# GEMM2 in products of 256 columns, with moving operands 192 bytes beyond the loaded ones

## The chip, the cores and the metric

The kernel runs on one core of one Trainium2 chip. The metric is device time in microseconds for one execution; the median of three runs of the kernel before is 678.66 us (678.33 to 679.98).

## What is computed

Sliding-window attention with sink tokens feeds a two-layer network with a leaky activation. All tensors are float32.

```
scores = q @ k.T / sqrt(64)                      # 4 batches, 8 heads, 768 tokens, head_dim 64
keep   = (key < 4) | (0 <= query - key < 128)    # 4 sink tokens, a window of 128
a      = softmax(where(keep, scores, -1e9))
x      = (a @ v), heads side by side             # 3072 tokens x 512
h      = x @ w_in                                # 512 -> 2048      (GEMM1)
g      = max(h, 0) + alpha * min(h, 0)
out    = g @ w_out                               # 2048 -> 512      (GEMM2)
```

## The kernel before, in words

The 3072 tokens are cut into twelve chunks of 256 (`QC`), three to a batch. For each chunk the attention gives x transposed, features on partitions; it is then taken through the network in sixteen blocks of the hidden layer (`f`, 0 to 15, 128 hidden features each). To keep float32 accuracy with matmuls of a rounded float32 type, every operand is split into a high part and a low part, and a product is the sum of three: high by high, high by low, low by high.

GEMM1 of a block (`gemm1`, matmul at L901) works in four steps of 128 input features. Each step has three products: a 128x128 block of the weights is loaded into TensorE, and 256 columns of x (`xh` or `xl`, 256 tokens) stream past it. Twelve products add up to h in one PSUM bank. ScalarE scales it by alpha (L905), VectorE takes the maximum (L906), ScalarE makes the high part `gh` (L907), VectorE the low part `gl` (L908).

GEMM2 (`gemm2`, L913 on) comes two blocks later. For it g is the loaded operand and the weights stream: for each half `j` of the chunk's tokens a 128x128 block of `gh` or `gl` is loaded, and the block's `w_out` (512 columns, its high part L938 and L936, its low part L939) streams past. There are six products of 512 columns to a block: `gh` by high and `gh` by low for both halves, then, when `gl` is ready, `gl` by high for both. The results accumulate in two PSUM banks over the sixteen blocks. The last block of the last chunk has the same six in another order (L923 to L925), half by half, so that the first output can leave early. After the sixteenth block ScalarE copies each bank to SBUF (L944) and a DMA on SP's queue stores it.

Each product has a load of its own, also where two in a row use the same block: the profile has as many loads as products.

The attention of the next chunk is spread over the blocks of the current one: the scores (L604, L605: 260 columns, 132 in a batch's first tiles) of one head and one half of the queries at a time, the softmax on VectorE and ScalarE, the products with v (L793, L882) towards the end. In the last chunk only the network is left.

The order of all instructions is planned beforehand (`Plan.draw`). An operation is declared by `op(engine, cost, run, reads, writes)`; the planner simulates the engines with these costs, picks each engine's order, and `Plan.emit` chains the instructions of an engine in that order. The cost of a matmul is `mm(columns)`, 0.456 ns a column, and GEMM2 is declared as two operations, of four and of two products of 512 columns.

Where tiles lie: `const` and `main` are pools without rotation that lay tiles one after another, in the order in which they are first asked for, rounded up to 32 bytes. So the sizes of tiles set the addresses of those behind. The size of the tile that holds one block's weights is `ROWS` words: first the split w_in (2 x 512 words), then `HALF` words of padding, then the split w_out. The sixteen weight tiles are in `const`; `gh`, `gl`, `vs`, `kq`, the padding tile `half` and then `xh`, `xl` follow in `main`. The tile `size` is the first of all; the weight tile of f = 14 lies right behind it, ahead of a group of small tiles (896 bytes together), the other fifteen behind those. `kq` holds q high, q low, `HALF` words of padding, and k.

With the kernel's first tile at byte 8320, the addresses modulo 512 come to:

| operand | before |
|---|---|
| w_in of f = 0, 3, 7, 11 | 384 |
| w_in of f = 1, 5, 9 | 128 |
| w_in of f = 2, 6, 10, 14, 15 | 256 |
| w_in of f = 4, 8, 12, 13 | 0 |
| w_out | w_in + 64 |
| gh, gl | 128 |
| xh, xl | 448 |
| q high, q low in the two kq | 128, 256 |
| k | q + 64 |

Steps inside an operand (256 or 128 columns, the four feature steps, high and low part) are multiples of 512 bytes.

Of the kernel before, what the change touches and what calls it, by code (L numbers as in the profile page):

```python
# [9 lines left out]
F32 = mybir.dt.float32  # L10
# [9 lines left out]
P = 128  # L20
B, H, S, D = 4, 8, 768, 64
DM, DF = 512, 2048
NS = 4
WIN = 2 * P + NS
QC = 2 * P
KC = 3 * P + 2 * NS
HALF = 16
KQ = 2 * QC + HALF + KC + HALF // 2
ROW = 2 * DM + HALF
ROWS = 2 * ROW  # L30
CPB = S // QC
NCHUNK = B * CPB
NF = DF // P
# [49 lines left out]
class Plan:  # L83
# [20 lines left out]
    def held(self, tile_):  # L104
        v = Value(None)
        v.at = tile_
        return v

    def op(self, engine, cost, run, reads=(), writes=(), tail=0.09, mode=None, nbytes=0, other=None, locks=False):
        o = Op(engine, cost, tail, run, self.rank if engine == "PE" else None)  # L110
        o.ways = {engine: (cost, run)}
        if other:
            o.ways[other[0]] = other[1:]
        o.born = self.rank
        if engine == "PE":
            self.rank += 1
        o.mode, o.nbytes, o.index = mode, nbytes, len(self.ops)
        seen = []
        for group, writing in ((reads, False), (writes, True)):
            for x in group:  # L120
                v, key = x if isinstance(x, tuple) else (x, None)
                if v not in seen:
                    seen.append(v)
                keys = [k for k in set(v.wrote) | set(v.read) if key is None or k is None or k == key]
                for k in keys:
                    o.before.update(v.wrote.get(k, ()))
                    if writing:
                        o.before.update(v.read.get(k, ()))
                if writing:
                    for k in keys:  # L130
                        if key is None or k == key:
                            v.wrote.pop(k, None)
                            v.read.pop(k, None)
                    v.wrote.setdefault(key, []).append(o)
                else:
                    v.read.setdefault(key, []).append(o)
        for v in seen:
            v.left += 1
        o.values = seen
        o.takes = [v for v in seen if v.kind]  # L140
        o.locks = locks
        self.ops.append(o)
        return o
# [148 lines left out]
def cast(n, psum=False):  # L292
    return (0.045 if psum else 0.092) + 0.84e-3 * n
# [18 lines left out]
def mm(n):  # L312
    return 0.456e-3 * n
# [12 lines left out]
def program(ctx, tc, qk, pairs, vp, vq, vs, w, par, out):  # L326
    nc = tc.nc
    const = ctx.enter_context(tc.tile_pool(name="const", bufs=1))
# [10 lines left out]
    def several(name, n, shape, dtype):  # L339
        plan.kind(name, [pool.tile(shape, dtype, name=f"{name}{i}") for i in range(n)])  # L340
# [7 lines left out]
    several("vs", 1, [P, DM], F32R)  # L348
    several("kq", 2, [P, KQ], F32R)
    pool.tile([P, HALF], F32, name="half")  # L350
    several("xh", 2, [P, KT, QC], F32R)
# [13 lines left out]
    several("jk", 3, [P, 2], F32)  # L365
    several("ts", 1, [P, 2, 4, 32], F32R)

    size = const.tile([P, 2 * NF], F32, name="size")[:, :NF]
    sizes = held(size)
    raws, fins = {}, {}  # L370

    def load_weights(f, engine="ACT"):
        raw = raws[f] = held(None)

        def run():
            raw.at = const.tile([P, ROWS], I32, tag=f"w{f}", name="wraw")[:, :2 * ROW].rearrange("p (i x) -> p i x", i=2)[:, :, :2 * DM]
            (nc.sync if engine == "SP" else nc.scalar).dma_start(
                raw.at, w[f].bitcast(I32).rearrange("i p x -> p i x"))
        return op(engine, ISSUE if engine == "SP" else 0.12, run, writes=[raw] + lent.get(f, []), nbytes=8 * P * 2 * DM)

    def convert_weights(f):
# [23 lines left out]
        def high_part(engine):  # L405
            fin.at = const.tile([P, ROWS], F32R, tag=f"w{f}", name=f"w{f}")[:, :2 * ROW].rearrange(
                "p (i x) -> p i x", i=2)[:, :, :2 * DM].rearrange("p i (a x) -> p i a x", a=2)
            (nc.scalar.copy if engine == "ACT" else nc.vector.tensor_copy)(fin.at[:, :, 0], wf())
# [68 lines left out]
    part, alt = param[:, :4], param[:, 4:].bitcast(F32)  # L477
# [81 lines left out]
    def prep_head(c, h):  # L559
# [5 lines left out]
        kq = val("kq")  # L565
        ks, qh, ql = [lambda s=s: kq.at[:, s] for s in (slice(2 * QC + HALF, 2 * QC + HALF + KC), slice(0, QC), slice(QC, 2 * QC))]
        q_raw, k_raw = lambda: st.at[:, :QC], lambda: st.at[:, QC:]
# [345 lines left out]
    def gemm2(c, f, dst):  # L913
        gh, gl = gs.pop((c, f))
        fin = fins[f]
        if f == 0:
            acc[c] = [val("pa"), val("s")] if c == 1 else [val("o"), val("o")]
        o2 = acc[c]
        if c == NCHUNK - 1 and f == NF - 1:
            for j in range(2):  # L920
                def last(j=j):
                    js = slice(j * P, (j + 1) * P)
                    nc.tensor.matmul(o2[j].at, gh.at[:, js], fin.at[:, 1, 0], start=False, stop=False)  # L923
                    nc.tensor.matmul(o2[j].at, gh.at[:, js], fin.at[:, 1, 1], start=False, stop=False)
                    nc.tensor.matmul(o2[j].at, gl.at[:, js], fin.at[:, 1, 0], start=False, stop=True)  # L925
                op("PE", 3 * mm(DM), last, reads=[fin, gh, gl], writes=[o2[j]], tail=R_TAIL)
                ob = val("ob")
                op("ACT", cast(DM, True), lambda ob=ob, j=j: nc.scalar.copy(ob.at, o2[j].at), reads=[o2[j]], writes=[ob])
                op("ACT", 0.1, lambda ob=ob, j=j: nc.scalar.dma_start(dst(j), ob.at), reads=[ob], nbytes=4 * P * DM)
            return  # L930
        for lowpart in range(2):
            def some(lowpart=lowpart):
                for j in range(2):
                    js = slice(j * P, (j + 1) * P)
                    if lowpart:
                        nc.tensor.matmul(o2[j].at, gl.at[:, js], fin.at[:, 1, 0], start=False, stop=(f == NF - 1))  # L936
                    else:
                        nc.tensor.matmul(o2[j].at, gh.at[:, js], fin.at[:, 1, 0], start=(f == 0), stop=False)  # L938
                        nc.tensor.matmul(o2[j].at, gh.at[:, js], fin.at[:, 1, 1], start=False, stop=False)  # L939
            op("PE", (2 if lowpart else 4) * mm(DM), some, reads=[fin, gl if lowpart else gh], writes=o2, tail=R_TAIL)  # L940
        if f == NF - 1:
            for j in range(2):
                ob = val("ob")
                op("ACT", cast(DM, True), lambda ob=ob, j=j: nc.scalar.copy(ob.at, o2[j].at), reads=[o2[j]], writes=[ob])  # L944
                op("SP", ISSUE, lambda ob=ob, j=j: nc.sync.dma_start(dst(j), ob.at), reads=[ob], nbytes=4 * P * DM)
            del acc[c]
# [112 lines left out]
    def dst(c):  # L1059
        return lambda j: out[c * QC + j * P:c * QC + (j + 1) * P]  # L1060
# [11 lines left out]
    for n, (c, f) in enumerate(order):  # L1072
        convert(f + 2)
        if (c, f) == (NCHUNK - 1, NF // 2):
            judge()
        gemm1(c, f)
        pend.append((c, f))
        todo = work[n]
        cut = round(len(todo) / 2)
        for st in todo[:cut]:  # L1080
            st()
        if len(pend) > LAG:
            gemm2(*pend[0], dst(pend.pop(0)[0]))
        for st in todo[cut:]:
            st()
    for a in pend:
        gemm2(*a, dst(a[0]))
# [197 lines left out]
```

## Time and profile before

| | |
|---|---|
| median of three runs | 678.66 us |
| profiled execution | 678.67 us, its span 676.7 us |
| TensorE products | 664.0 us busy (98%), 4534 |
| TensorE loads | 580.2 us busy (86%), 4534 |
| VectorE | 525.9 us busy (78%) |
| ScalarE | 397.5 us busy (59%) |
| GEMM1 products (L901), 256 columns | 2304 |
| GEMM2 products (L936, L938, L939, L923 to L925), 512 columns | 1152 |

A row of the timeline gives the start in microseconds from the span's start, the length, the engine and line, what is written and read, the shape, and how many instructions in a row were merged. PE is TensorE's products and PEld its loads. Products overlap, so the length of a row is not what a product costs; the difference of the starts of two products in a row is. A row of the windows gives, for each engine, the busy time and the number of instructions in that stretch, then the granted clock and what the DMAs did.

### The profile page before, as it was taken

The page shows a single profiled execution, that of the slowest core. Times are in us where ns is not written, and L with a number is a line of the kernel's source. Part 1 is how long each engine was busy: PE and PEld are TensorE (multiplying, and loading weights), DVE is VectorE, ACT ScalarE, POOL GpSimd, SP SyncE. Part 2 cuts the span into 40 slices and gives each one's busy share as a digit, 9 for nine tenths or more (in the row PEclk, how much of TensorE's full clock was granted, in tenths as well). Part 3 has the DMA queues.
Part 4 walks back from the last instruction along what each step waited for, and adds up shares of the span by engine and source line. Part 5 has one row for each costly group of instructions (what it writes and reads, how often), then busy time and mean ns, then how long its engine had stood idle before and what let it go on. Part 6 is the DMA issues. An engine that isn't in the chain of part 4 may idle for free.

```text
span 676.7 us, 13245 instructions
## 1 busy us (share of the span) xinstructions
PE 664.0 (98%) x4534; PEld 580.2 (86%) x4534; DVE 525.9 (78%) x1750; ACT 397.5 (59%) x1066; POOL 34.6 (5%) x115
## 2 busy tenths in 40 slices
PE   9989999999999999999999999999999999999996
PEld 4568898888989989989988988988998988998995
DVE  6999999968967977986986985995895994994331
ACT  6989888827537627736636735744744753853332
POOL 2110000001000000010000000010000000000000
PEclk9989999999999999999999999999999999999999
DMA  8674641325343453442434433542542543420001
GB/s 313 238 278 163 244 162 44 122 75 155 118 125 107 127 144 105 139 133 88 141 118 118 142 112 92 157 139 61 173 127 77 161 127 89 141 93 18 32 2 35
DMA packets 58683, 85.19 MB, mean 126 GB/s; under 512 B 9072, under 2 KB 35056, under 8 KB 58608
## 3 DMA queue, kind: packets, MB, share of 16 engines
q1 hardware_dynamic: 55056, 71.17, 34.5%
q10 hardware_dynamic: 3552, 13.11, 5.3%
q8 instruction: 37, 0.61, 0.4%
q14 instruction: 38, 0.31, 0.2%
HBM read 67.22 MB, written 17.04 MB: 125 GB/s over the span
## 4 chain that ended last, share of the span: by engine, by line
PE 83%; DVE 9%; ACT 5%; issue 2%; POOL 0%; DMA 0%; ACTq 0%; SPq 0%; POOLq 0%
PE bank L901 35%; PE bank L938 12%; PE bank L936 11%; PE bank L939 11%; PE bank L793 3%; PE bank L605 3%; PE bank L604 3%; PE bank L882 2%; DVE wa L402 2%; ACT pt L621 1%; ACT wa L388 1%; DVE wa L400 1%; DVE w L411 1%; DVE g L906 1%; DVE gl L908 1%
## 5 line engine op out<-in xcount | busy, mean ns | idle before, releaser
L901 PE MATMUL bank<-xh,w 128*128 128x256 f32 x1536 | 307.8, 282 | 0.4 <-DVE g L906 0.2
L901 PEld LDWEIGHTS bank<-xh,w 128*128 128x128 f32 x1536 | 250.2, 189 | 9.5 <-DVE g L906 3.2
L901 PE MATMUL bank<-xl,w 128*128 128x256 f32 x768 | 215.1, 280 | 0.1
L905 ACT ACTIVATE g<-bank,param 128x256 f32<-128x256 f32 x192 | 90.4, 471 | 117.6 <-PE bank L901 112.2
L938 PE MATMUL bank<-w,gh 128*128 128x512 f32 x382 | 151.5, 397 | 0.2 <-ACT gh L907 0.2
L939 PE MATMUL bank<-w,gh 128*128 128x512 f32 x382 | 150.4, 394 | 0.0
L901 PEld LDWEIGHTS bank<-xl,w 128*128 128x128 f32 x768 | 145.1, 189 | 4.4 <-DVE xl L815 0.3
L621 ACT ACTIVATE pt<-pt,nm 128x260 f32<-128x260 f32 (+1 forms) x192 | 94.5, 493 | 53.4 <-DVE nm L617 52.9
L936 PE MATMUL bank<-w,gl 128*128 128x512 f32 x382 | 120.2, 396 | 0.0
L906 DVE TENSOR_TENSOR g<-bank,g 128x256 f32<-128x256 f32 x192 | 79.7, 419 | 51.1 <-ACT g L905 50.3
L907 ACT CAST gh<-g 128x256 fp32r<-128x256 f32 x192 | 77.0, 404 | 60.8 <-DVE g L906 60.6
L908 DVE TENSOR_TENSOR gl<-g,gh 128x256 fp32r<-128x256 f32 x192 | 80.4, 423 | 26.5 <-ACT gh L907 23.0
L617 DVE CUSTOM_DVE_ANT_0 pt<-bank,masks 128x260 f32<-128x260 f32 (+1 forms) x192 | 74.9, 401 | 19.7 <-PE bank L605 16.2
L936 PEld LDWEIGHTS bank<-w,gl 128*128 128x128 f32 x382 | 70.8, 188 | 16.3 <-issue 0.7
L938 PEld LDWEIGHTS bank<-w,gh 128*128 128x128 f32 x382 | 72.0, 188 | 9.5 <-ACT gh L907 0.6
L939 PEld LDWEIGHTS bank<-w,gh 128*128 128x128 f32 x382 | 71.9, 188 | 8.2
L570 DVE TENSOR_TENSOR kq<-stage,kq 64x392 fp32r<-64x392 f32 x80 | 45.3, 566 | 2.7
L666 POOL TENSOR_TENSOR sink<-pt,ri 128x8 f32<-128x8 f32 x80 | 20.8, 264 | 505.7 <-DVE ri L651 382.8
L604 PE MATMUL bank<-kq 128*128 128x260 f32 (+1 forms) x160 | 44.5, 278 | 1.2 <-DVE nm L617 1.2
L605 PE MATMUL bank<-kq 128*128 128x260 f32 (+1 forms) x160 | 45.1, 282 | 0.0
L662 DVE CUSTOM_DVE_ANT_0 comb<-pt,ri 128x128 f32<-128x128 f32 x136 | 43.2, 343 | 0.4
L568 ACT CAST kq<-stage 128x392 fp32r<-128x392 f32 x80 | 41.0, 512 | 0.7 <-PE bank L605 0.2
(130 smaller groups left out, 685.0 us busy)
## 6 DMA issues: line engine op xcount, KB each, us to landing
stage<-qk SPq DMA_DIRECT2D x80, 324.0 KB, 3.0
wraw<-w ACTq DMA_DIRECT2D x12, 1024.0 KB, 5.2
swap<-comb SPq DMA_DIRECT2D x36, 256.0 KB, 2.1
comb<-swap SPq DMA_DIRECT2D x36, 256.0 KB, 3.3
v<-vq SPq DMA_DIRECT2D x36, 192.0 KB, 2.6
out_dram<-ob SPq DMA_DIRECT2D x22, 256.0 KB, 3.5
wraw<-w SPq DMA_DIRECT2D x4, 1024.0 KB, 11.2
v<-vp SPq DMA_DIRECT2D x8, 192.0 KB, 7.0
```

The lines of the kernel that those rows point to most:

```text
L604: nc.tensor.matmul(s[:, w0], qh()[:, qs], ks()[:, kw], start=True, stop=False)
L605: nc.tensor.matmul(s[:, w0], ql()[:, qs], ks()[:, kw], start=False, stop=True)
L617: op("DVE", dve(n), lambda: nc.vector.tensor_tensor_reduce(out=pt.at[:, u, w0], in0=s.at[:, w0], in1=masks[:, i, w0], scale=-0.125, scalar ...
L621: op("ACT", exp(n), lambda: nc.scalar.activation(pt.at[:, u, w0], pt.at[:, u, w0], AF.Exp, bias=nm.at[:, h, u:u + 1], scale=-1.0, accum_ou ...
L901: nc.tensor.matmul(h(), fin.at[:, 0, part, ks], rhs.at[:, kt], start=(kt == 0 and n == 0), stop=(kt == KT - 1 and n == 2))
L905: op("ACT", act(QC, True), lambda: nc.scalar.activation(g.at, h(), AF.Copy, scale=alt[:, f:f + 1]), reads=[bk, known("param")], writes=[g])
L906: op("DVE", dve(QC), lambda: nc.vector.tensor_tensor(g.at, h(), g.at, ALU.max), reads=[bk], writes=[g])
L907: op("ACT", cast(QC), lambda: nc.scalar.copy(gh.at, g.at), reads=[g], writes=[gh])
L908: op("DVE", dve(QC), lambda: nc.vector.tensor_tensor(gl.at, g.at, gh.at.bitcast(F32), ALU.subtract), reads=[g, gh], writes=[gl])
L936: nc.tensor.matmul(o2[j].at, gl.at[:, js], fin.at[:, 1, 0], start=False, stop=(f == NF - 1))
L938: nc.tensor.matmul(o2[j].at, gh.at[:, js], fin.at[:, 1, 0], start=(f == 0), stop=False)
L939: nc.tensor.matmul(o2[j].at, gh.at[:, js], fin.at[:, 1, 1], start=False, stop=False)
```

## The change

Two things are changed together.

GEMM2's products of 512 columns are each made as two of 256, one after the other, into the two halves of the same PSUM bank. Both load the same block of `gh` or `gl`. Only the very first product into a bank carries the start flag, and the last one of a pair the stop flag. The operations, their costs in the plan and so their order stay.

The padding changes. `HALF` goes from 16 to 48 words, so w_out lies 192 bytes beyond w_in, modulo 512, and k 192 bytes beyond q; the padding tile `half` ahead of `xh` grows with it. `ROWS` goes from 2080 words (8320 bytes, 16 x 512 + 128) to 2176 (8704 bytes, 17 x 512). `KQ` goes from 928 to 960 words, 7.5 x 512 bytes. `size` grows by 256 bytes. The addresses modulo 512 become:

| operand | after |
|---|---|
| w_in of fifteen f | 384 |
| w_in of f = 14 | 0 |
| w_out | w_in + 192 |
| gh, gl | 384 |
| xh, xl | 64 |
| q high, q low in the two kq | 384, 128 |
| k | q + 192 |

```diff
-HALF = 16
-KQ = 2 * QC + HALF + KC + HALF // 2
+HALF = 48
+KQ = 2 * QC + HALF + KC + 8
 ROW = 2 * DM + HALF
-ROWS = 2 * ROW
+ROWS = 4 * DM + P
...
-    size = const.tile([P, 2 * NF], F32, name="size")[:, :NF]
+    size = const.tile([P, 6 * NF], F32, name="size")[:, :NF]
...
         o2 = acc[c]
+        halves = [slice(n * QC, (n + 1) * QC) for n in range(2)]
+
+        def product(j, gx, part, stop=False):
+            js = slice(j * P, (j + 1) * P)
+            for n, hs in enumerate(halves):
+                nc.tensor.matmul(o2[j].at[:, hs], gx.at[:, js], fin.at[:, 1, part, hs], start=(f == 0 and gx is gh and not part and not n), stop=stop and n == 1)
         if c == NCHUNK - 1 and f == NF - 1:
             for j in range(2):
                 def last(j=j):
-                    js = slice(j * P, (j + 1) * P)
-                    nc.tensor.matmul(o2[j].at, gh.at[:, js], fin.at[:, 1, 0], start=False, stop=False)
-                    nc.tensor.matmul(o2[j].at, gh.at[:, js], fin.at[:, 1, 1], start=False, stop=False)
-                    nc.tensor.matmul(o2[j].at, gl.at[:, js], fin.at[:, 1, 0], start=False, stop=True)
+                    product(j, gh, 0)
+                    product(j, gh, 1)
+                    product(j, gl, 0, True)
...
                 for j in range(2):
-                    js = slice(j * P, (j + 1) * P)
                     if lowpart:
-                        nc.tensor.matmul(o2[j].at, gl.at[:, js], fin.at[:, 1, 0], start=False, stop=(f == NF - 1))
+                        product(j, gl, 0, f == NF - 1)
                     else:
-                        nc.tensor.matmul(o2[j].at, gh.at[:, js], fin.at[:, 1, 0], start=(f == 0), stop=False)
-                        nc.tensor.matmul(o2[j].at, gh.at[:, js], fin.at[:, 1, 1], start=False, stop=False)
+                        product(j, gh, 0)
+                        product(j, gh, 1)
```

## The prediction

> **What bounds the kernel now.** I read the page's busy times first, then the chain that ended last, then TensorE's own waits.
>
> ```profile
> PE 664.0 (98%) x4534; PEld 580.2 (86%) x4534; DVE 525.9 (78%) x1750; ACT 397.5 (59%) x1066; POOL 34.6 (5%) x115
> PE 83%; DVE 9%; ACT 5%; issue 2%; POOL 0%; DMA 0%; ACTq 0%; SPq 0%; POOLq 0%
> ```
> ```profile
> PE bank L595 <- DVE nm L617: 2.2, 2, 1.2
> ...
> PE bank L901 <- DVE g L906: 0.2, 1, 0.2
> PE bank L938 <- ACT gh L907: 0.2, 1, 0.2
> ```
>
> TensorE is busy for 98% of the span, its waits are a few tenths of a microsecond per line, and DVE (78%) and ACT (59%) have room. So from about 60 us on the time is the sum of the product-to-product steps on TensorE, and the question is how long one step is. The windows before and after 60 us give the counts that matter.
>
> ```profile
> 0.00:60.00 60.00, 54.89 (x338) 36.08 (x339) 52.31 (x147) 50.56 (x128) 9.37 (x32) 0.97 0.70 253
> 60.00:676.70 616.70, 609.13 (x4199) 544.09 (x4197) 473.59 (x1604) 346.93 (x939) 25.25 (x83) 1.00 0.37 114
> ...
> 60.00:676.70 616.70, 296.54 (x2232) 281.57 (x2232) 1.00 0.37 114
> ...
> 60.00:676.70 616.70, 148.11 (x374) 70.48 (x374) 1.00 0.37 114
> ```
>
> The first two rows are all engines; the third is L901 alone (GEMM1, 2232 products of 256 columns), the fourth L938 alone (374 products of 512 columns). L939 and L936 have as many, so GEMM2 has 1122 there. Granted clock: 1.00.
>
> The busy mean of a product (some 280 and 396 ns) overlaps its neighbours; the step is the difference of two starts. A stretch of the last chunk, with nothing but the two GEMMs, shows it:
>
> ```profile
> 630.62 0.39 PE L938 MATMUL bank<-w,gh 128*128 128x512 f32 x1
> ...
> 631.99 0.28 PE L901 MATMUL bank<-xh,w 128*128 128x256 f32 x1
> ...
> 633.35 0.39 PE L938 MATMUL bank<-w,gh 128*128 128x512 f32 x1
> ```
>
> Six products of 512 columns take 631.99 - 630.62 = 1.37 us, 228 ns each; twelve of 256 take 1.36 us, 113.3 ns each. Other blocks of the same shape are slower. Here are two executions of the same block, f = 15, in two chunks, by the start of the first and the start of what follows the twelfth:
>
> ```profile
> 463.05 0.28 PE L901 MATMUL bank<-xh,w 128*128 128x256 f32 x1
> ...
> 464.41 0.39 PE L938 MATMUL bank<-w,gh 128*128 128x512 f32 x1
> ```
> ```profile
> 410.08 0.28 PE L901 MATMUL bank<-xh,w 128*128 128x256 f32 x1
> ...
> 411.49 0.40 PE L938 MATMUL bank<-w,gh 128*128 128x512 f32 x1
> ```
>
> 1.36 us against 1.41 us: 113 or 117.5 ns a step. I took the steps of all 2176 GEMM1 products after 60 us that no break follows (the first and last of the 2232 are those of the windows above). They fall into two heaps with little between: a fast step of mean 113.5 ns and a slow one of mean 118.0. A block mostly settles within four products on one and stays there to its end. 61% are slow, the mean is 116.2. The 512-wide steps lie at 225 to 238 ns, mean 231.8: the same two speeds, by halves (2 x 113.5 = 227, 2 x 118 = 236).
>
> **What the speed goes with.** While one product streams its moving operand, the next one's stationary block is loaded. With tile sizes as written, the start of the moving operand minus that of the next load, modulo 512 bytes, follows by arithmetic. In GEMM1 X moves and W loads: a weight tile is 8320 = 16 x 512 + 128 bytes, so that distance takes four values over the sixteen f. GEMM1 means after 60 us, slow share behind them:
>
> | X minus W, modulo 512 | products | mean step, ns | slow |
> |---|---|---|---|
> | 64 | 541 | 117.1 | 82% |
> | 192 | 688 | 115.7 | 48% |
> | 320 | 399 | 117.7 | 96% |
> | 448 | 548 | 115.0 | 31% |
>
> The two f = 15 blocks above are both of the 192 row; one block of the 320 row, f = 1, and one of the 448 row, f = 4:
>
> ```profile
> 362.94 0.28 PE L901 MATMUL bank<-xh,w 128*128 128x256 f32 x1
> ...
> 364.36 0.28 PE L604 MATMUL bank<-kq 128*128 128x260 f32 x1
> ```
> ```profile
> 372.76 0.28 PE L901 MATMUL bank<-xh,w 128*128 128x256 f32 x1
> ...
> 374.12 0.28 PE L604 MATMUL bank<-kq 128*128 128x260 f32 x1
> ```
>
> 1.42 us against 1.36. So the distance sways which speed a block settles on, and does not fix it. In the 192 row, from a block's fifth product on, 62% are fast; between its third and eleventh product ten steps go from slow to fast and none from fast to slow.
>
> The Trainium skill says otherwise: "SBUF — State Buffer", section "Who interferes with whom", gives TensorE two independent read ports, one for the moving operand and one for loads, and has TensorE never wait on anyone. By it the four rows would be alike, and they are not (96% against 31% slow). I go by the rows and keep that rule as a rival.
>
> **The change, part by part.**
>
> *Distances.* A weight tile becomes 8704 = 17 x 512 bytes, so W has one residue for fifteen f; GEMM1 then has X 192 beyond W, GEMM2 has W_out 192 beyond the gh and gl blocks, scores have k 192 (and 208) beyond q. The tile of f = 14 is laid down ahead of the small tiles, at another residue: there GEMM1 has 64 and GEMM2 has 320, both slow rows. This adds no instruction; copies and DMAs keep shapes and order.
>
> GEMM1, fifteen f: 2232 x 15/16 = 2092 products. Bounds from the two heaps: all fast (113.5 - 116.2) x 2092 = -5.7 us; all slow (118.0 - 116.2) x 2092 = +3.8. I take the settled share of the 192 row, 62% fast: 0.62 x 113.5 + 0.38 x 118.0 = 115.2, that is -1.0 ns each, -2.1 us. GEMM1, f = 14: from the 192 row's 115.7 to a slow 118: 140 x 2.3 = +0.3 us.
>
> *GEMM2 in halves.* 1122 products of 512 become 2244 of 256, and as many loads. That the loads keep up is shown by GEMM1, which issues a load and a product every 113 ns, and by the loads around a 132-wide score:
>
> ```profile
> 310.95 0.19 PEld L605 LDWEIGHTS bank<-kq 128*128 128x128 f32 x1
> 311.05 0.19 PEld L901 LDWEIGHTS bank<-xh,w 128*128 128x128 f32 x1
> 311.16 0.19 PEld L901 LDWEIGHTS bank<-xl,w 128*128 128x128 f32 x1
> ```
>
> Loads follow each other at 0.10 to 0.11 us. A 256-wide step is just above that, so the load hides, with 3 to 13 ns to spare; without that cover the step would be the load's. A pair of halves costs 227 ns fast, 236 slow, 2 x 115.2 = 230.4 at the share taken, against 231.8: -1.4 ns for 1052 products (fifteen f), -1.5 us; bounds (227 - 231.8) x 1052 = -5.0 and (236 - 231.8) x 1052 = +4.4. f = 14: 70 x 4.2 = +0.3 us.
>
> The Trainium skill, "TensorE: Matmul & The Clock Gate", section "Wait — 56ns, not 53.3ns?", gives each matmul a fixed cost of about 2.5 ns beyond its columns, which speaks against halving: as an estimate from that page, 1122 x 2.5 = 2.8 us more. The fast rows (1.36 us for twelve halves' worth, 1.37 for six wholes) do not show it; by that rule the sum below would be 2.8 us higher.
>
> *The rest.* The 320 score products keep their count; single steps are 115 to 124 ns, mean about 120, so at most 320 x 4 = 1.3 us either way; I take 0. The order of operations is planned from costs that the change leaves alone: nothing is moved past a queue, no wait is added. If TensorE gains, DVE and ACT get the same work in about 1% less time, at 78% and 59%. The first 60 us (x72 of L901, x8 of L938) wait for loads and softmax and give nothing.
>
> *Sum:* -2.1 + 0.3 - 1.5 + 0.3 = -3.0 us. The profiled execution took 678.67 us around a span of 676.7; the median of the runs is 678.66, so the sum stands against either: 675.6 us.
>
> **Rivals.**
>
> 1. *Fast throughout.* One distance everywhere and one width, so a stream that once settles fast is not thrown out by 512-wide products. For it: no step from fast to slow in the middle of the 192 row. Against: slow runs of that row last twelve products too, and scores and values still break the stream. -5.7 - 5.0 + 0.6 = -10.1: 668.6 us.
>
> 2. *Slow throughout, the other side.* The place in memory may count beside the distance. In the 192 row X started at 448 modulo 512; now every moving operand starts at 64 (f = 14's W_out apart) and loads at 384, which no GEMM1 row has. If that place holds the stream slow, as the 320 row is, it costs (118.0 - 116.2) x 2232 = +4.0 us in GEMM1 and 4.2 x 1122 = +4.7 in GEMM2: 687.4 us. For it: the 512-wide products at distance 192 were the slowest class now, 232.6 ns against 231.1 to 231.9. It decides from the share at which 2232 x (s - 116.2) + 1122 x (2s - 231.8) is zero: s = 116.05, 57% slow; above that the kernel is slower than before.
>
> 3. *The layout does nothing.* The speeds go with what came before a block and not with addresses, as the skill's rule on ports would have it. GEMM1 stays at 116.2; halves cost 2 x 116.2 = 232.4, +0.6 x 1122 = +0.7 us: 679.4. For it: the same f = 15 block at the same distance runs at both speeds. Against: the 96% and 31% rows.
>
> **How the numbers follow.** A measurement of this kernel tells about 0.3% (2 us) from no change: faster is below 676.6, slower above 680.7. Forecast (a mixture, 48 to 75% fast, 678.4 to 673.1 us): 0.40, of which 0.28 faster and 0.12 same. Rival 1: 0.23, faster. Rival 3: 0.15, of which 0.13 same and 0.02 slower. Rival 2: 0.22, slower. Together faster 0.51, same 0.25, slower 0.24. The forecast's own range is 673 to 678.5; the one for 8 times in 10 reaches to rival 1 (667) and to most of the way to rival 2 (685).
>
> **What would show it.** In the changed kernel: two GEMM2 rows where there was one, 113 to 118 ns apart; GEMM1 blocks of twelve between 1.36 and 1.42 us with more than 60% at 1.36; f = 14's blocks slow. The forecast is wrong if the 256-wide steps take a third value, if more than 57% are slow, or if pairs of halves cost more than 236 ns, which would mean loads or issue no longer hide; then TensorE's loads would show gaps of more than 0.11 us that its products do not.

## The result, and the profile after

The changed kernel takes 681.85 us (median of 16 runs, 680.89 to 684.79) against 678.61 us for the kernel before (16 runs). The ratio is 1.0053, 95% interval 1.0041 to 1.0064: slower by half a percent, 3.2 us, where 675.6 us was forecast. The spread of the runs goes with the granted clock: the changed kernel's runs at 0.999 to 1.000 have a median of 680.9 us and those at 0.993 and 0.994 one of 683.3, and the kernel before spreads alike (678.0 and 680.2 us in the series of `layout_only`).

The page of the changed kernel, busy times, chain and waits of TensorE:

```profile
span 680.9 us, 15549 instructions
PE 667.7 (98%) x5686; PEld 637.0 (94%) x5686; DVE 526.4 (77%) x1750; ACT 399.0 (59%) x1066; POOL 34.5 (5%) x115
PE 83%; DVE 8%; ACT 5%; issue 2%; DMA 0%; POOL 0%; ACTq 0%; SPq 0%; POOLq 0%
```
```profile
PE bank L595 <- DVE nm L617: 2.2, 2, 1.2
...
PE bank L924 <- ACT gh L907: 0.3, 1, 0.3
```

TensorE bounds it as before. Its waits are those of before and one of 0.4 us in the first 5 us (L595, for a DMA). 1152 products and loads have been added and the other engines do the same work. The windows from 60 us on, for L901 (GEMM1) and L924 (GEMM2) alone, give the counts:

```profile
60.00:680.90 620.90, 297.34 (x2232) 275.32 (x2232) 1.00 0.37 113
...
60.00:680.90 620.90, 296.46 (x2256) 278.06 (x2256) 1.00 0.37 113
```

What changed is the step from one product's start to the next. The steps lie in the same two heaps as before, near 113.5 and near 118 ns, and more of them are slow: 71% in GEMM1 (mean 116.5 ns, 61% and 116.2 before), 79% in GEMM2's halves (mean 116.9 ns, so 233.7 a pair, against 231.8 for a product of 512 columns). That is 0.3 x 2232 = 0.7 us in GEMM1 and 1.9 x 1122 = 2.1 us in GEMM2, 2.8 of the 3.2 us.

The last chunk shows best how. From its GEMM1 of f = 0 to that of f = 7 nothing but the two GEMMs runs: seven blocks, 84 products of 256 columns and 42 of 512 before, 168 of 256 after. Rows of the timeline, first product of f = 0 and of f = 7, before:

```profile
623.64 0.28 PE L901 MATMUL bank<-xh,w 128*128 128x256 f32 x1
...
643.05 0.28 PE L901 MATMUL bank<-xh,w 128*128 128x256 f32 x1
```

and after:

```profile
627.04 0.28 PE L901 MATMUL bank<-xh,w 128*128 128x256 f32 x1
...
646.82 0.28 PE L901 MATMUL bank<-xh,w 128*128 128x256 f32 x1
```

19.41 us before, 19.78 after: 117.7 ns a step. Of these 168 steps of the changed kernel one is fast. Before, the seven GEMM1 blocks of the same stretch are at either speed: those of f = 0, 1 and 5 slow, those of f = 2, 3, 4 and 6 fast but for a step at most.

### The profile page after: what moved, and what is told of

The parts are those of the page before. It is cut to its first block, busy times and chain, and to the rows that moved or that the text cites. A ratio compares the mean times of both kernels' runs of the same rounds, so it can differ in the third digit from the quotient of the medians.

```text
span 680.9 us, 15549 instructions
## 1 busy us (share of the span) xinstructions
PE 667.7 (98%) x5686; PEld 637.0 (94%) x5686; DVE 526.4 (77%) x1750; ACT 399.0 (59%) x1066; POOL 34.5 (5%) x115
## 4 chain that ended last, share of the span: by engine, by line
PE 83%; DVE 8%; ACT 5%; issue 2%; DMA 0%; POOL 0%; ACTq 0%; SPq 0%; POOLq 0%
PE bank L901 35%; PE bank L924 35%; PE bank L793 3%; PE bank L605 3%; PE bank L604 3%; PE bank L882 2%; DVE wa L402 2%; ACT pt L621 1%; ACT wa L388 1%; DVE wa L400 1%; DVE w L411 1%; DVE g L906 1%; DVE gl L908 1%; PE bank L866 1%; DVE pt L617 1%
## 5 line engine op out<-in xcount | busy, mean ns | idle before, releaser
L901 PE MATMUL bank<-xh,w 128*128 128x256 f32 x1536 | 308.7, 283 | 0.4
L901 PEld LDWEIGHTS bank<-xh,w 128*128 128x128 f32 x1536 | 250.8, 189 | 3.1 <-issue 1.5
L901 PE MATMUL bank<-xl,w 128*128 128x256 f32 x768 | 215.4, 280 | 0.1
L924 PE MATMUL bank<-w,gh 128*128 128x256 f32 x1536 | 211.6, 280 | 0.3 <-ACT gh L907 0.3
L924 PEld LDWEIGHTS bank<-w,gh 128*128 128x128 f32 x1536 | 193.7, 189 | 1.2 <-ACT gh L907 0.5
L905 ACT ACTIVATE g<-bank,param 128x256 f32<-128x256 f32 x192 | 90.9, 474 | 121.0 <-PE bank L901 117.4
L901 PEld LDWEIGHTS bank<-xl,w 128*128 128x128 f32 x768 | 145.6, 190 | 0.3 <-DVE xl L815 0.3
L924 PE MATMUL bank<-w,gl 128*128 128x256 f32 x768 | 121.6, 280 | 0.0
L924 PEld LDWEIGHTS bank<-w,gl 128*128 128x128 f32 x768 | 103.5, 189 | 0.7 <-issue 0.7
L621 ACT ACTIVATION_READ_ACCUMULATOR pt<-pt,nm 128x1 f32 x192 | 36.2, 188 | 0.0
L572 DVE TENSOR_TENSOR kq<-stage,kq 128x256 fp32r<-128x256 f32 x80 | 34.9, 436 | 1.3
```

Of the source, the lines that this page charges most:

```text
L621: op("ACT", exp(n), lambda: nc.scalar.activation(pt.at[:, u, w0], pt.at[:, u, w0], AF.Exp, bias=nm.at[:, h, u:u + 1], scale=-1.0, accum_ou ...
L901: nc.tensor.matmul(h(), fin.at[:, 0, part, ks], rhs.at[:, kt], start=(kt == 0 and n == 0), stop=(kt == KT - 1 and n == 2))
L905: op("ACT", act(QC, True), lambda: nc.scalar.activation(g.at, h(), AF.Copy, scale=alt[:, f:f + 1]), reads=[bk, known("param")], writes=[g])
L924: nc.tensor.matmul(o2[j].at[:, hs], gx.at[:, js], fin.at[:, 1, part, hs], start=(f == 0 and gx is gh and not part and not n), stop=stop an ...
```

## The experiments

Shares and means are taken as in the prediction: steps after 60 us, start to start, without those that a break follows (a step over 140 ns, over 260 for 512 columns); slow is a step over 115 ns. The shares come from one profiled execution of each kernel. Ratios are to the kernel before on the same chip, with 95% intervals.

| kernel | median, us | ratio | GEMM1 mean, ns (slow) | GEMM2 mean, ns (slow) |
|---|---|---|---|---|
| changed | 681.85 | 1.0053 (1.0041 to 1.0064) | 116.5 (71%) | 116.9 (79%) |
| layout_only | 679.48 | 1.0016 (1.0007 to 1.0026) | 116.3 (66%) | 232.1 for 512 |
| halves_only | 679.52 | 1.0015 (1.0006 to 1.0024) | 116.3 (62%) | 116.4 (68%) |
| place_256 | 681.53 | 1.0046 (1.0030 to 1.0061) | 116.9 (79%) | 117.2 (86%) |
| distance_448 | 679.12 | 1.0014 (0.9999 to 1.0028) | 115.5 (46%) | 116.1 (60%) |
| distance_0 | 691.36 | 1.0191 (1.0161 to 1.0220) | 119.4 | 119.3 |
| distance_256 | 692.24 | 1.0204 (1.0174 to 1.0233) | 119.5 | 119.8 |
| distance_384 | 690.63 | 1.0180 (1.0147 to 1.0214) | 119.0 | 118.8 |
| cuts | 679.43 | 1.0017 (1.0005 to 1.0028) | 115.3 (42%) | 116.4 (55%), equal halves |
| cut_4 | 679.12 | 1.0014 (1.0002 to 1.0026) | 115.6 (48%) | 116.8 (77%), equal halves |
| cut_4_448 | 677.50 | 0.9992 (0.9979 to 1.0005) | 115.1 (35%) | 115.8 (55%), equal halves |
| f14_same | 677.18 | 0.9979 (0.9968 to 0.9989) | 115.7 (52%) | 115.8 (55%) |
| wide_448 | 678.75 | 1.0003 (0.9990 to 1.0016) | 115.7 (50%) | 232.4 for 512 |
| place_128 | 682.83 | 1.0059 (1.0040 to 1.0078) | 116.6 (73%) | 116.9 (79%) |
| f14_448 | 675.46 | 0.9954 (0.9937 to 0.9971) | 114.8 (30%) | 115.3 (42%) |
| f14_448_cut | 675.75 | 0.9958 (0.9943 to 0.9973) | 114.8 (29%) | 115.4 (46%), equal halves |
| f14_wide | 679.12 | 1.0005 (0.9991 to 1.0019) | 116.2 (62%) | 232.3 for 512 |
| f14_320 | 683.34 | 1.0072 (1.0055 to 1.0089) | 117.4 (90%) | 117.8 (98%) |
| f14_448_scores | 675.74 | 0.9962 (0.9947 to 0.9978) | 114.9 (31%) | 115.3 (42%) |

**The two halves of the change, one at a time.** `layout_only` is the kernel before with the new padding:

```diff
-HALF = 16
-KQ = 2 * QC + HALF + KC + HALF // 2
+HALF = 48
+KQ = 2 * QC + HALF + KC + 8
-ROWS = 2 * ROW
+ROWS = 4 * DM + P
-    size = const.tile([P, 2 * NF], F32, name="size")[:, :NF]
+    size = const.tile([P, 6 * NF], F32, name="size")[:, :NF]
```

> The new padding alone, GEMM2 still in products of 512 columns. Theory (a stream of one width keeps the speed on which it settled, and a change of width gives it a chance to leave it; with halves the slow speed lasted): the 512-wide products between GEMM1's blocks break the stream as before, so GEMM1 goes back to about the 48% slow of the 192 row, 115.7 ns mean (116.5 in the changed kernel), and the 512-wide step is that of the 192 class, 232.6 ns; time 677 to 680 us, no slower than before. Rival A (the new addresses hold the stream slow whatever the width): GEMM1 stays about 70% slow, 116.5 ns, the 512-wide steps rise towards 234 to 236 ns; 681 to 684 us.

`halves_only` has GEMM2's `product` of the changed kernel and these four lines as they were.

> GEMM2 in halves with the old padding, four distances over the sixteen f. Theory (halves let the slow speed last): slow shares of GEMM1 rise above the 61% of before and pairs of halves cost more than the 231.8 ns of a 512-wide product, near 234; 680 to 684 us. Rival A (the addresses did it): GEMM1 as before, 116.2 ns, pairs of halves 2 x 116.2 = 232.4; 679 us, within 0.3% of before.

Each alone costs about 0.15%, both together 0.53%. With 512-wide products between them GEMM1's blocks at 192 bytes are 64% slow (2048 steps), not the 48% of the row before; with halves between them, in `halves_only`, the same row is 32% slow (688 steps) while GEMM2's halves are 68% slow. So the share of a row is no property of its distance: it moves by tens of points with what runs around it. The two runs don't decide between the theory and rival A. Of `layout_only` the theory's time came out, but not its 48%, and rival A's time did not; of `halves_only` rival A's figures came out (116.3 ns in GEMM1, 2 x 116.4 = 232.9 a pair, 679.5 us), and the theory's 680 to 684 us did not.

**The place.** `place_256` moves every address behind the first tile by 256 bytes and keeps all distances.

```diff
-    size = const.tile([P, 6 * NF], F32, name="size")[:, :NF]
+    size = const.tile([P, 2 * NF], F32, name="size")[:, :NF]
```

> The changed kernel with the first tile at its old size, so that every address behind it moves by 256 bytes and all distances stay. Theory (distance and history set the speed): the same slow shares as in the changed kernel, about 70% in GEMM1 and 79% in GEMM2, 681 to 683 us. Rival B (the place modulo 512 counts): shares differ by 15 points or more, 5 us or more either way between 667 and 687 us.

1.0046 against 1.0053: the intervals overlap, and the time is in the range that the theory gave. The shares are 7 or 8 points higher, short of the 15 that rival B named. The place modulo 512 is not what made the changed kernel slow.

**Other distances.** The distance of GEMM1's and GEMM2's moving operands is set to 448, 0, 256 and 384 bytes by the padding, with all weight tiles at 8704 bytes as in the changed kernel (the view of a tile takes its two parts by `ROW`, so that the second may reach to the tile's end). The scores keep 192, but for `distance_0`, where they have 0 too. The core of `distance_448`:

```diff
-HALF = 48
-KQ = 2 * QC + HALF + KC + 8
+HALF = 112
+KQ = 952
+KH = 48
...
-    pool.tile([P, HALF], F32, name="half")
...
-        ks, qh, ql = [lambda s=s: kq.at[:, s] for s in (slice(2 * QC + HALF, 2 * QC + HALF + KC), slice(0, QC), slice(QC, 2 * QC))]
+        ks, qh, ql = [lambda s=s: kq.at[:, s] for s in (slice(2 * QC + KH, 2 * QC + KH + KC), slice(0, QC), slice(QC, 2 * QC))]
```

> The changed kernel with 448 bytes in place of 192 for GEMM1 and GEMM2 (scores keep 192). In the kernel before, the 448 row was 31% slow. Theory that the distance sways which speed is settled on: slow share under 45% in both GEMMs, mean step under 115.5 ns, 671 to 676 us. Rival C (history alone): slow share as in the changed kernel, 70 to 79%, 681 to 683 us.

> The changed kernel with no bytes in place of 192, for GEMM1, GEMM2 and scores: moving and loaded operands start at the same residue. Theory (distance sways, history picks): still the same two steps, 113.5 and 118 ns, with another share; 667 to 690 us. If two reads of one place disturb each other most when they start together: steps above 118 ns, over 690 us. If distance does nothing: 70 to 79% slow, 681 to 683 us.

> The changed kernel with 256 bytes in place of 192 for GEMM1 and GEMM2. The same two steps of 113.5 and 118 ns with another share, 667 to 690 us, by the theory; 70 to 79% slow and 681 to 683 us if distance does nothing.

> The changed kernel with 384 bytes in place of 192 for GEMM1 and GEMM2. The same two steps of 113.5 and 118 ns with another share, 667 to 690 us, by the theory; 70 to 79% slow and 681 to 683 us if distance does nothing.

The distance counts, and more than the rows of before could show, which had only 64, 192, 320 and 448: at 0, 256 and 384 most steps are 117 to 121 ns, and the kernel is 1.8 to 2.0% slower (two runs of each). The commonest step of GEMM1 is 120 ns there (1397, 1301 and 572 of some 2180), a value that 40 of 2176 steps have in the kernel before. So the theory's "same two steps" and its range up to 690 us failed at all three; at 0 the other case, steps above 118 ns and over 690 us, came out. The stretch of the last chunk at distance 0:

```profile
633.88 0.28 PE L904 MATMUL bank<-xh,w 128*128 128x256 f32 x1
...
654.01 0.28 PE L904 MATMUL bank<-xh,w 128*128 128x256 f32 x1
```

20.13 us, 119.8 ns a step, against 19.78 at 192. The programs have the same products and loads, TensorE's waits are alike to some tenths of a microsecond, and the other engines are busy for the same time to within 2 us. Some 8.6 us lie between distances 192 and 384 (1.0053 against 1.0180, the difference times 678.6). The Trainium skill's "SBUF — State Buffer", section "Who interferes with whom", gives TensorE two independent read ports and has it wait on no one; the runs at 192 and 384 do not agree with that, though none shows what in TensorE takes the longer. At 448 the kernel is better than at 192 (1.0014), with 46 and 60% slow, but not the 45% or less in both that was expected: in its last chunk 93% of GEMM1 is slow, as at 192.

**Something unequal in the stream.** In `cuts` the first pair of each GEMM2 block is cut unevenly, by another amount for each f; in `cut_4` at 260 and 252 columns throughout; `cut_4_448` has the same at 448 bytes.

```diff
+KICKS = (4, 8, 12, 16, 20, 24, 28, 32, 40, 48, 64, 96, 128, -16, -32, -64)
...
         halves = [slice(n * QC, (n + 1) * QC) for n in range(2)]
+        cut = QC + KICKS[f]
+        kicked = [slice(0, cut), slice(cut, DM)]
...
-            for n, hs in enumerate(halves):
+            for n, hs in enumerate(kicked if gx is gh and not part and not j else halves):
```

> The changed kernel, with one pair of GEMM2 products in each block (the first: half j = 0, gh by the high part) cut unevenly, at 256 + d columns, d = 4, 8, 12, 16, 20, 24, 28, 32, 40, 48, 64, 96, 128, -16, -32, -64 for f = 0 to 15; all the rest is 256 wide. Theory (a stream of equal products keeps its speed until something unequal comes): in the last chunk, where the changed kernel ran slow from f = 15's GEMM2 of the chunk before to f = 14's GEMM1 without one fast block, the speed now changes at several of the cuts and holds from one cut to the next; total 675 to 683 us. Rival A (the addresses hold it slow): the last chunk stays slow up to f = 14; 681 to 683 us.

The last chunk of `cuts` is slow through the cuts of f = 12, 13 and 14 of the chunk before, runs two slow products behind that of f = 15 (192 and 320 columns), turns fast, and from then on every GEMM1 block of f = 2 to 7 runs its twelve products fast. Behind each further cut of 4 to 20 columns the stream runs three to five slow products and is fast again; behind d = 24 and d = 40 it stays slow for the rest of the GEMM2 block, and behind d = 40 through the GEMM1 block that follows too. So a speed lasts until something unequal comes, and what comes decides the next one: this is the theory's case, and the time is in its range. The same stretch:

```profile
624.17 0.28 PE L902 MATMUL bank<-xh,w 128*128 128x256 f32 x1
...
643.54 0.28 PE L902 MATMUL bank<-xh,w 128*128 128x256 f32 x1
```

19.37 us with seven uneven pairs in it.

> The changed kernel (192 bytes), with the first pair of every GEMM2 block cut at 260 and 252 columns, every other pair at 256. Theory (a stream of equal products keeps its speed; something unequal lets it leave the slow one): slow share in GEMM1 falls from 70% to 30 to 45%, in the equal halves of GEMM2 from 79% to 45 to 60%, and the last chunk is fast in all GEMM1 blocks soon after its start; with 15 ns a block for the uneven pair and what follows it, 672 to 677 us. Rival A (the addresses hold the stream slow): shares as in the changed kernel, 681 to 684 us.

> The same uneven first pair, with 448 bytes in place of 192. Theory: as with 192 or better by what the distance gives (GEMM1 46% slow without the cut): GEMM1 20 to 40% slow, 669 to 676 us. If the cut works at one distance alone: as 448 without it, 678 to 680 us.

Both are faster than without the cut (1.0014 against 1.0053, 0.9992 against 1.0014), but by less than was expected (679.1 and 677.5 us). In `cut_4` GEMM1 is 48% slow, in the last chunk 49%, where it was to be fast soon after the start, and GEMM2's equal halves stay at 77%: in the chunks with scores the cut at 4 columns does not bring GEMM2 to the fast speed.

**One tile.** f = 14's weight tile lies ahead of the small tiles and so at another residue than the other fifteen; three of its products are the last before GEMM2 of f = 12 starts the stretch behind the products with v. `f14_same` widens one small tile, so that f = 14 has the distances of the rest. All places behind it move by 128 bytes with it. `place_128` moves the places by as much, f = 14's too, and so leaves f = 14's distances as they were.

```diff
-    flag = const.tile([1, 1], I32, name="flag")
+    flag = const.tile([1, 33], I32, name="flag")[:, :1]
```
```diff
-    size = const.tile([P, 6 * NF], F32, name="size")[:, :NF]
+    size = const.tile([P, 8 * NF], F32, name="size")[:, :NF]
```

> The changed kernel with 128 bytes more among the small tiles, so that the weight tile of f = 14 has the residue of the others. Theory (something unequal lets the stream leave a speed): the last chunk, slow up to f = 14 in the changed kernel and fast behind it, now has no such place and keeps one speed to its end; total within 2 us of the changed kernel, 680 to 684 us. Rival (f = 14's own distances were a cost): f = 14's blocks, 93 to 100% slow, come down to the others' share and the total falls by 0.4 us.

> The changed kernel with 128 bytes more in the first tile: every address behind it, f = 0's to the last, lies where it does in f14_same, and only f = 14's weight tile keeps its own residue. If f = 14's distances made the difference in f14_same: slow as the changed kernel, last chunk slow from its start, 680 to 684 us. If the place made it: as f14_same, 676 to 678 us.

`f14_same` is 4.7 us faster than the changed kernel, and faster than the kernel before (0.9979). That the last chunk keeps one speed to its end was right; that the total would stay was wrong, because the speed it keeps is the fast one. The rival's 0.4 us was too little by far. With the places of `f14_same` and f = 14's distances as they were, `place_128` is as slow as the changed kernel. So it is f = 14's distances. The way in, in the changed kernel: the last products with v, three of GEMM1's f = 14, twelve of GEMM2's f = 12, then GEMM1 of f = 15.

```profile
622.01 0.39 PE L882 MATMUL bank<-comb,v 128*64 128x128 f32 x4
622.33 0.39 PE L901 MATMUL bank<-xh,w 128*128 128x256 f32 x1
...
622.80 1.10 PE L924 MATMUL bank<-w,gh 128*128 128x256 f32 x8
623.74 0.63 PE L924 MATMUL bank<-w,gl 128*128 128x256 f32 x4
624.21 0.28 PE L901 MATMUL bank<-xh,w 128*128 128x256 f32 x1
```

The same in `f14_same`, and its stretch from f = 0 to f = 7:

```profile
618.02 0.39 PE L882 MATMUL bank<-comb,v 128*64 128x128 f32 x4
618.34 0.39 PE L901 MATMUL bank<-xh,w 128*128 128x256 f32 x1
...
618.80 1.07 PE L924 MATMUL bank<-w,gh 128*128 128x256 f32 x8
619.71 0.62 PE L924 MATMUL bank<-w,gl 128*128 128x256 f32 x4
620.16 0.28 PE L901 MATMUL bank<-xh,w 128*128 128x256 f32 x1
...
622.88 0.28 PE L901 MATMUL bank<-xh,w 128*128 128x256 f32 x1
...
641.92 0.28 PE L901 MATMUL bank<-xh,w 128*128 128x256 f32 x1
```

Twelve halves take 624.21 - 622.80 = 1.41 us in the changed kernel, 620.16 - 618.80 = 1.36 us here, and their speed is kept for some 26 us, up to a single small transpose ahead of GEMM1 of f = 8; four products behind it the stream is back at that speed. From f = 0 to f = 7 it takes 19.04 us, 113.3 ns a step. In `place_128` the stretch is

```profile
624.79 0.28 PE L901 MATMUL bank<-xh,w 128*128 128x256 f32 x1
...
644.58 0.28 PE L901 MATMUL bank<-xh,w 128*128 128x256 f32 x1
```

19.79 us, 117.8 ns. In the last chunk's GEMM1, 93% is slow in the changed kernel and in `place_128`, and 2% in `f14_same`.

The same break stands in the chunks before. Behind f = 14's last products follow GEMM2 of f = 12, GEMM1 of f = 15, GEMM2 of f = 13, GEMM1 of the next f = 0 and GEMM2 of f = 14, before the next scores. For chunks 1 to 10 (counted from 0) the 591 steps of these five blocks add up to 69.51 us in the changed kernel and in `place_128` (95% slow), and to 67.14 us in `f14_same` (6% slow). The other steps of the last chunk add up to 43.37, 43.37 and 41.95 us. That is 2.4 and 1.4 of the 4.7 us between the changed kernel and `f14_same`; all other steps of the two GEMMs together differ by 0.1 us. f = 14's own GEMM1 blocks stay 81% slow in `f14_same`, so its own products are not where the gain lies.

**Both together, and 512 columns again.** `f14_448` is `distance_448` with the wider small tile; `f14_448_cut` adds the cut at 260 and 252 in all chunks but the last. `wide_448` and `f14_wide` have the paddings of `distance_448` and `f14_same` with GEMM2 in products of 512.

> 448 bytes in place of 192 and f = 14's weight tile at the residue of the others. Theory (where no operand is unequal, the stream holds the speed with which it leaves the products with v; with f = 14 equal that is the fast one): last chunk fast throughout, GEMM1 slow share of distance_448 (46%) down to 25 to 35%, GEMM2's 60% to 40 to 50%; 673 to 677 us. If f = 14 matters at 192 alone: 678 to 680 us.

> As f14_448, with the first pair of GEMM2's blocks cut at 260 and 252 columns in all chunks but the last. Theory: the cut helps where the scores leave GEMM2 slow and costs about 15 ns a block where the stream is fast; GEMM1 slow share 20 to 30%, 673 to 676 us, not over f14_448 by more than 1 us.

> GEMM2 in products of 512 columns, 448 bytes in place of 192. Theory that what comes before a block counts beside the distance: GEMM1 slow share between 30 and 60%, 512-wide steps near 231.5 ns; 675 to 679 us. Rival C (distance alone): GEMM1 31% slow as in the 448 row of before, -1.3 ns x 2232 = -2.8 us and no change in GEMM2; 675.8 us.

> The padding of f14_same with GEMM2 in products of 512 columns. Theory (products of one width let a speed last; 512-wide ones break it): the last chunk is no longer fast throughout, GEMM1 40 to 65% slow, 512-wide steps 231 to 233 ns; 677.5 to 680.5 us. Rival (the equal distances alone gave the gain): last chunk fast as in f14_same, 674 to 677.5 us.

`f14_448` takes 675.46 us, 0.9954 of the kernel before (0.9937 to 0.9971): it beats both kernels, and its time and shares are in the ranges that the theory gave. Its last chunk is fast but for a few steps behind the transpose ahead of f = 8:

```profile
621.52 0.28 PE L904 MATMUL bank<-xh,w 128*128 128x256 f32 x1
...
640.56 0.28 PE L904 MATMUL bank<-xh,w 128*128 128x256 f32 x1
```

The cut adds nothing to it. With 512 columns the same paddings are no better than the kernel before (1.0003 and 1.0005, both times in the theory's range). In `f14_wide` the last chunk's GEMM1 blocks are fast but for their first product (10% slow, where 40 to 65% was expected), so 512-wide products do not put GEMM1 out, as the theory had it; they are what is slow themselves. One block of it, its GEMM2 and the GEMM1 that follows:

```profile
625.48 0.39 PE L938 MATMUL bank<-w,gh 128*128 128x512 f32 x1
...
626.87 0.28 PE L901 MATMUL bank<-xh,w 128*128 128x256 f32 x1
```

Six products in 1.39 us, 232 ns each, against two fast halves in `f14_same`'s 226.7 (1.36 us for twelve). Halving gains where the stream is fast (`f14_same` against `f14_wide`, 0.9979 against 1.0005) and loses where it is slow (the changed kernel against `layout_only`, 1.0053 against 1.0016; a pair of slow halves takes 2 x 117.7 = 235 ns).

**The slowest row, and the scores.** `f14_320` is `f14_same` at 320 bytes; `f14_448_scores` is `f14_448` with k 448 bytes beyond q (`KH = 112`, `KQ = 1016`). Both have the first tile at its old size, to fit.

> As f14_same with 320 bytes in place of 192 and the first tile at its old size. 320 was the slowest row before (96% slow). If the distance holds a stream slow by itself: the last chunk slow throughout, GEMM1 over 85% slow, 683 to 687 us. If only the way in counts: the last chunk all one speed, as like as not the fast one, and a share of 45 to 75% elsewhere; 676 to 682 us.

> As f14_448, with k 448 in place of 192 bytes beyond q, so that the scores too have the distance of the GEMMs, and the first tile at its old size. Theory (the scores between the blocks decide with which speed the next block starts): last chunk as in f14_448, fast; the shares of the chunks with scores move, either way, by 10 points or more; 672 to 679 us. If the scores' own distance does nothing: as f14_448, 675.5 us.

At 320 nearly everything is slow, the last chunk without exception:

```profile
627.45 0.28 PE L905 MATMUL bank<-xh,w 128*128 128x256 f32 x1
...
647.24 0.28 PE L905 MATMUL bank<-xh,w 128*128 128x256 f32 x1
```

19.79 us. But 10% of GEMM1's steps are fast, and they come in whole blocks: in chunks 6 and 9 eight blocks each are fast in all twelve products. One of them, up to the score that follows it:

```profile
371.52 0.28 PE L905 MATMUL bank<-xh,w 128*128 128x256 f32 x1
...
372.88 0.28 PE L608 MATMUL bank<-kq 128*128 128x260 f32 x1
```

1.36 us. So 320, too, allows both speeds, as 192 and 448 do; it has the fast one seldom. Moving k from 192 to 448 bytes beyond q changes nothing: shares and time are those of `f14_448`. That theory fell. With or without it the chunks with scores go through the same round of blocks, some slow from end to end and some fast from the third or fourth product on.

## Why the prediction was wrong

*TensorE's steps are the time; two steps, 113.5 and 118 ns:* right. The steps of the changed kernel are in the same heaps, and 2.8 of the 3.2 us are read from them.

*Distances sway the speed:* right, and stronger than the four rows told (0, 256 and 384 are a class of their own, 320 is mostly slow in unbroken stretches too).

*"I take the settled share of the 192 row, 62% fast":* this step failed, and with it the sign. The share was taken from blocks of twelve between products of 512 columns and blocks at other distances. It is not a property of 192: with the same distance GEMM1 was 32% slow in `halves_only`, 48% before, 64% in `layout_only`, 70% in the changed kernel and 52% in `f14_same`. (Counted over all 456 steps from the fifth product on, the share itself is 59% fast; with it the sum would have been -2.4 us in place of -3.0, of the same sign.) In a stream of equal products a speed lasts from one break to the next, so the mean is set by which speed the breaks leave behind, and the few breaks of the changed kernel mostly leave the slow one. In the last chunk one break decided the next 26 us.

*f = 14, "+0.3 us" in each GEMM:* right for its own products (117.5 and 118.0 ns), and mis-sized by what it does to others, which the sum left out. Equal distances for f = 14 alone were worth 4.7 us, 3.8 of them in the blocks behind f = 14 and in the last chunk.

*GEMM2 in halves:* that loads and issue hide was right; a pair costs 226.7 ns where fast. It was priced at the same wrong share. The estimate of 2.8 us for a fixed cost of each matmul is not borne out: with the padding of `f14_same` the halves are 1.8 us faster than the products of 512 columns (0.9979 against 1.0005, the difference times 678.6).

*Rival 1, no step from fast to slow in mid-stream:* the mechanism was real, and `f14_same` and `f14_448` show it in the last chunk, but it works for the slow speed as well. That slow stretches last too was named as an argument against it, and the price was that of the gain alone.

*Rival 2, the other side:* the sign came out and 57% slow as the point from which it decides was passed (71 and 79%). Its cause, the place in memory, did not hold: `place_256` and `place_128`.

*Rival 3, the layout does nothing:* fell with `distance_0` and `f14_same`.

## What to carry to other kernels

Where matmuls run back to back, take start-to-start steps and look whether they come in heaps that last; a mean over such heaps, or the share in a group, belongs to the order in which it was measured and is not a price for another order. In these kernels an edit that made the stream more uniform made whatever speed it entered with last, so check each place where the stream starts again, and each operand that lies differently from the rest: one odd tile was worth more here than the whole change. Distances of moving and loaded operands are worth a sweep on the chip that includes multiples of 128 bytes, to know what to stay away from.

## What the runs showed of the hardware

Equal products of 256 columns ran at 113.3 or at 117.7 ns a step, either one for over 25 us but for single steps, in kernels (`f14_same`, `place_128`) that differ in where the weight tile of f = 14 and the small tiles lie. With the moving operand 0, 256 or 384 bytes beyond the next load, modulo 512, most steps were 117 to 121 ns; at 320 90% of GEMM1's and 98% of GEMM2's were slow; at 192 and 448 both speeds were common. In `f14_same` the one change of speed in the middle of an unbroken stream comes with a single step of 135 ns, at 344.72 us, and the stream is slow from there to the next other operation, at 347.92 us; whether the long step made it so is not shown. What in the chip keeps the two speeds, and by what rule a break picks one, stays open: the shares in the chunks with scores (32% slow in GEMM1 and 46% in GEMM2 even in `f14_448`) hardly moved with the scores' distance (33 and 46%) or with the cut at 4 columns (31 and 51%). Distances 64 and 128 were not run as a whole.
